# One-token attention on one core: the first pair's odd keys and its values in one load each, and 88 instructions of TensorE ahead of its loop

## The chip, the cores and the metric

The kernel runs on one core of a Trainium2 chip. The metric is the device time of one execution in microseconds; the median of several runs is compared. Beside the runs there is one execution taken by the hardware profiler, and all durations below are from it. "Before" is the kernel without the change, "after" the one with it.

## The reference

Attention for one new token. There are 32 query heads, 8 key and value heads (four query heads share one), 65,536 tokens, and a head size of 128, all in bf16:

```python
def reference(q, k, v):
    B, Hq, Sq, D = q.shape
    Hkv = k.shape[1]
    rep = Hq // Hkv
    k = jnp.repeat(k, rep, axis=1)
    v = jnp.repeat(v, rep, axis=1)
    scale = D ** -0.5
    scores = jnp.einsum("bhqd,bhkd->bhqk", q, k) * scale
    p = _softmax(scores, axis=-1)
    return jnp.einsum("bhqk,bhkd->bhqd", p, v)
```

Keys and values are 134 MB each. Every byte of them is read once.

## The kernel before, in words

**Tiling.** A *unit* is a quarter of one key head's tokens, 16,384 of them, as 128 partitions with 128 tokens each. The 32 units are taken as 16 *pairs* (an even and an odd unit, n = 0 and 1); two pairs make a head. A pair has 8.4 MB of keys and 8.4 MB of values.

**TensorE** runs one hardware loop of 16 laps, a pair each (`tensor_engine`, L178; the pair's body is `pe_pair`, L165). Its instructions are written out in full inside the lap: for each unit 16 groups of eight 128x128 transposes of keys (`pe_transposes`, L132), three groups later that group's eight score matmuls (`pe_scores`, L141), and at the lap's end 128 value matmuls for each unit (`pe_values`, L159). That is 768 matmuls a lap, each with its weight load. The same code is executed in every lap, and SyncE hands out semaphore "tokens" (`tokens`, L404) where a lap has fewer loads than the code has waits. Ahead of the loop stand two waits, the transpose of the queries (L181) and one more wait.

**VectorE and ScalarE** copy each transposed group from PSUM to `ktb` (`evict`, L189 and following; three of four on VectorE, L202, the fourth on ScalarE, L200), find the unit's largest score, exponentiate the scores into `pts` (L342) and add up the results (`values_done`, L249). **GpSimd** finds maxima across partitions and, in most pairs, copies the odd unit's keys from `kbuf` to `bbuf` (L208).

**SyncE** issues every load of keys and values, in program order on one queue (`sync_engine`, L393). `kbuf` holds a pair's keys, `bbuf` the odd unit's copy, `vbuf` a pair's values, each once. So a pair's keys can be asked for when the pair before has been transposed out of `kbuf` (`kfree`), and its values when the pair before has used up `vbuf` (`vfree`, which VectorE raises after TensorE's last value matmul). In pairs 1 to 13 the keys are one load (L413) and the values one load (L436). In pair 0 the keys go in four: the even unit's two halves into `kbuf`, the odd unit's two halves into `bbuf` (`K_PIECES`, L402), each half with a semaphore of its own; the values go in two, one for each unit (L433). TensorE waits for each half at the transposes that begin it, and for each unit's values at the first of its value matmuls. The last two pairs are cut up in their own way, and the change leaves them as they are.

Of the kernel before, what the change touches and what calls it, by code (L numbers as in the profile page):

```python
# [14 lines left out]
NTB = 4  # L15
NKG = 8
LAG = 3
CB = 16
HU = 4
Q = 32  # L20
# [18 lines left out]
def starts(sizes):  # L39
    return [sum(sizes[:i]) for i in range(len(sizes))]  # L40


def take(e, sem, n=1):

    e.wait_ge(sem, n)
    e.sem_inc(sem, -n)  # L46


def bass_standalone__gqa_softmax__decode_kernel(nc, q, k, v, out):
    _, Hq, _, D = q.shape  # L50
    _, H, Sk, _ = k.shape
# [3 lines left out]
    NP = NU // 2  # L55
# [7 lines left out]
    def sb(name, shape, dt):  # L63
        return S(nc.sbuf_tensor(name, shape, dt))

    def sem(name):
        return S(nc.semaphore(name))
# [3 lines left out]
    vbuf = sb("vbuf", [P, 2 * T * D], DT.bfloat16)  # L71
# [34 lines left out]
    vp = [[sem(f"vp{i}_{p}") for p in range(len(V_PIECES[i]))] for i in range(2)]  # L106
# [5 lines left out]
    qkd, qrdy, pvd = sem("qkd"), sem("qrdy"), sem("pvd")  # L112
    cm, cma, ng, dmr, exd, sx, lrd, lra = (sem(n) for n in ("cm", "cma", "ng", "dmr", "exd", "sx", "lrd", "lra"))
    acr, l_sem, lws = sem("acr"), sem("l_sem"), sem("lws")
    xd, xa, xg = sem("xd"), sem("xa"), sem("xg")
    q_sem, o_sem, s_x, t_if, t_id, t_o, t_f, t_row = (
        sem(n) for n in ("q_sem", "o_sem", "s_x", "t_if", "t_id", "t_o", "t_f", "t_row"))

# [5 lines left out]
    def pe_transposes(pe, n, j):  # L124
        kv = (bbuf if n else kbuf)[:, 0:T * D].rearrange("p (t d) -> p t d", d=D)
        if j * TB in starts(K_PIECES[n]):
            take(pe, kp[n][starts(K_PIECES[n]).index(j * TB)], 16)
        if n and j * TB % CB == 0:
            take(pe, cpa if j * TB // CB in sum(ACT_COPIES.values(), ()) else cpg)
        for i in range(TB):  # L130
# [4 lines left out]
    def pe_scores(pe, n, j):  # L135
        take(pe, eva if on_act(j) else evd)
        if n == 0 and j == 0:
            take(pe, qrdy)
        for i in range(TB):
            t, off = j * TB + i, (j % NKG * TB + i) * P  # L140
            ins = pe.matmul(qkb[n][:, t * R:(t + 1) * R], lhsT=ktb[:, off:off + P],  # L141
                            rhs=qcur[:, :], start=True, stop=True)
        if j == G - 1:
            ins.then_inc(qkd, 1)
# [20 lines left out]
    def pe_pair(pe, lap):  # L165
        pend = []
        for n in range(2):
            for j in range(G):
                pe_transposes(pe, n, j)
                pend.append((n, j))  # L170
                if len(pend) > LAG:
                    pe_scores(pe, *pend.pop(0))
        while pend:
            pe_scores(pe, *pend.pop(0))
        for n in range(2):
            pe_values(pe, n, lap)

    def tensor_engine(pe):  # L178
        pe.wait_ge(q_sem, 16)
        pe.wait_ge(t_id, 1)  # L180
        pe.transpose(qps[:, 0:HR], qsb[:, :], ident[0:HR, 0:HR]).then_inc(s_x, 1)  # L181
        pe.wait_ge(t_if, 1)
        with pe.Fori(0, NP) as lap:
            pe_pair(pe, lap)
        pe.wait_ge(t_f, H)
        pe.transpose(trb[0][0:R, 0:P], oT[:, HR - R:HR], ident[:, :]).then_inc(s_x, 1)  # L186
# [17 lines left out]
    def copy_unit(e, cond, copies, op, done, x):  # L204
        with e.If(cond):
            for c in copies:
                off = T * D + c * CB * D
                ins = op(bbuf[:, c * CB * D:(c + 1) * CB * D], kbuf[:, off:off + CB * D])  # L208
                if c != copies[-1]:
# [183 lines left out]
    def sync_engine(e):  # L393
        W = T * D

        def src(x, p):
            h, c = p // 2, p % 2
            return x[h, c * 2 * P * T:(c + 1) * 2 * P * T, :].rearrange("(p t) d -> p (t d)", p=P)

        def pieces(to, s, sizes, sems):  # L400
            for a, w, sm in zip(starts(sizes), sizes, sems):
                e.dma_start(to[:, a * D:(a + w) * D], s[:, a * D:(a + w) * D]).then_inc(sm, 16)  # L402

        def tokens(sems):  # L404
            for sm in sems:
                e.sem_inc(sm, 16)

        for p in range(NP):
            ks, vs = src(kf, p), src(vf, p)
            if p:  # L410
                e.wait_ge(kfree, 3 * p)
            if WHOLE[0] <= p < WHOLE[1]:
                e.dma_start(kbuf[:, :], ks).then_inc(kp[0][0], 16)  # L413
                tokens(kp[0][1:])
            else:
                for n in range(2):
                    if n and p:
                        e.wait_ge(bfree, p)
                    to, s = bbuf if n else kbuf, ks[:, n * W:(n + 1) * W]
                    if p == 0 or (p == NP - 1 and n == 0):  # L420
                        pieces(to, s, K_PIECES[n], kp[n])
                    else:
                        e.dma_start(to[:, 0:W], s).then_inc(kp[n][0], 16)
                        tokens(kp[n][1:])
                e.sem_inc(cpg, len(POOL_COPIES))
                e.sem_inc(cpa, len(sum(ACT_COPIES.values(), ())))
            if p:
                e.wait_ge(vfree, p)
            if WHOLE[0] <= p < WHOLE[1]:
                tokens(kp[1])  # L430
            if p == 0:
                for n in range(2):
                    e.dma_start(vbuf[:, n * W:(n + 1) * W], vs[:, n * W:(n + 1) * W]).then_inc(vp[n][0], 16)  # L433
                tokens(vp[1][1:])
            elif p < NP - 1:
                e.dma_start(vbuf[:, :], vs).then_inc(vp[0][0], 16)  # L436
                tokens(vp[1])
            else:
                for n in range(2):
                    pieces(vbuf[:, n * W:(n + 1) * W], vs[:, n * W:(n + 1) * W], V_PIECES[n], vp[n])  # L440
        e.wait_ge(t_o, H)
        for b, rows in enumerate(OUT_ROWS):
            for r, n in zip(starts(rows), rows):
                e.dma_start(of[r:r + n, b * Q:(b + 1) * Q],
                            orow[b * Q + r:b * Q + r + n, :]).then_inc(o_sem, 16)
        e.wait_ge(t_row, 1)
        e.dma_start(of[HR - R:HR, :], lrow[:, :]).then_inc(l_sem, 16)

    with nc.Block() as block:
        block.tensor(tensor_engine)  # L450
        block.vector(vector_engine)
        block.scalar(scalar_engine)
        block.gpsimd(gpsimd_engine)
        block.sync(sync_engine)
# [30 lines left out]
```

## Time and profile before

| | us |
|---|---|
| median of 3 runs (lowest to highest) | 628.47 (628.29 to 628.52) |
| the profiled execution, its own time | 628.32 |
| its span, first to last instruction | 626.9 |
| TensorE busy with matmuls, all laps | 483.5 |
| VectorE busy | 315.1 |
| ScalarE busy | 229.1 |
| GpSimd busy | 159.9 |

How to read the lines that the prediction shows: the page's slices cut the span into 40 equal parts, and a digit is the busy share in tenths. A queue's row has its packets, megabytes and the share of 16 DMA engines' time. In a row of instructions in order of time stand the start, the length, the engine, the line, the operation, what it writes and reads, the count that was merged into the row, and in brackets how long the engine stood idle before it and what ended that; "issue" means that it waited for nothing that the profile shows, "PEq" that its own sequencer held it. A row of a stretch has, for each engine, the busy time and the number of instructions, then TensorE's granted clock, the share of the DMA engines, and GB/s. In a row of one line's instructions stand the shortest, median and longest duration in ns, and the first and last start. `PEldq` and `SPq` are the sequencers of TensorE and SyncE.

### The profile page before, as it was taken

The numbers are of one execution on the slowest core, as the hardware profiler recorded it, in microseconds if no ns is written. First come the engines' busy times: TensorE is split into PE (matmuls) and PEld (weight loads), VectorE is DVE, ScalarE is ACT, GpSimd is POOL, SyncE is SP. The second block draws the span as 40 slices with busy tenths as digits, with TensorE's granted clock in tenths as the row PEclk, the third lists the DMA queues.
The fourth block names the chain that finished last, engine by engine and source line by source line (L and its number), as shares of the span: only waits on it lengthen the run. The fifth ranks groups of instructions, "written<-read, shape, count | busy, mean of one in ns | idle before, by whom it ended". The sixth has DMA issues, their size and how long they took to land. (4 is left out here: it accounts for less than half of the span.)

```text
span 626.9 us, 27836 instructions
## 1 busy us (share of the span) xinstructions
PE 483.5 (77%) x12292; PEld 477.2 (76%) x12292; DVE 315.1 (50%) x699; ACT 229.1 (37%) x445; POOL 159.9 (25%) x124
## 2 busy tenths in 40 slices
PE   4753995949859598694976949679596894999798
PEld 4752995949859498694976949679596794999798
DVE  4530653717437174471744718346182561848274
ACT  2330542515335153340634407245071441624133
POOL 0000704307042070520605115060150702400000
PEclk9975886959869597795977959779596895969697
DMA  8999999999999999999999999999999999999997
GB/s 368 433 454 424 439 431 439 431 439 426 443 414 456 410 439 426 443 426 439 431 426 444 426 443 426 439 431 439 431 439 431 435 435 435 416 441 426 414 435 310
DMA packets 6424, 268.57 MB, mean 428 GB/s; under 512 B 912, under 2 KB 1040, under 8 KB 1168
## 3 DMA queue, kind: packets, MB, share of 16 engines
q1 hardware_dynamic: 6368, 268.45, 99.2%
q8 instruction: 6, 0.10, 0.1%
q10 hardware_dynamic: 48, 0.01, 0.0%
q14 instruction: 2, 0.02, 0.0%
HBM read 268.44 MB, written 0.01 MB: 428 GB/s over the span
## 5 line engine op out<-in xcount | busy, mean ns | idle before, releaser
L202 DVE COPY ktb<-trb 128x1024 bf16<-128x1024 bf16 x384 | 254.8, 689 | 178.2 <-PE trb L132 173.5
L200 ACT ACTIVATE ktb<-trb 128x1024 bf16<-128x1024 bf16 x128 | 131.1, 1024 | 352.4 <-PE trb L132 296.4
L132 PE MATMUL trb<-ident,kbuf 128*128 128x128 bf16 x2048 | 176.8, 244 | 104.7 <-PEq L46 104.7
L132 PEld LDWEIGHTS trb<-ident,kbuf 128*128 128x128 bf16 x2048 | 143.5, 110 | 105.7 <-issue 105.5
L208 POOL COPY bbuf<-kbuf 128x2048 bf16<-128x2048 bf16 x78 | 143.9, 1893 | 178.2 <-POOLq L46 178.2
L141 PE MATMUL qkb<-qcur,ktb 128*128 128x4 bf16 x4096 | 174.3, 165 | 12.5 <-PEq L46 10.0
L141 PEld LDWEIGHTS qkb<-qcur,ktb 128*128 128x128 bf16 x4096 | 155.7, 97 | 19.0 <-issue 19.0
L132 PE MATMUL trb<-ident,bbuf 128*128 128x128 bf16 x2048 | 156.9, 219 | 4.6 <-issue 4.0
L159 PE MATMUL pvb<-pts,vbuf 128*128 128x4 bf16 x4096 | 112.7, 166 | 14.9 <-issue 9.2
L159 PEld LDWEIGHTS pvb<-pts,vbuf 128*128 128x128 bf16 x4096 | 110.7, 102 | 16.4 <-issue 15.9
L132 PEld LDWEIGHTS trb<-ident,bbuf 128*128 128x128 bf16 x2048 | 117.3, 97 | 1.6 <-issue 1.6
L388 POOL PARTITION_ALL_REDUCE cmaxa<-cmax x32 | 11.8, 370 | 253.8 <-POOLq L46 253.8
L342 ACT ACTIVATE pts<-qkb,negm 128x128 bf16<-128x128 f32 x128 | 51.1, 552 | 37.2 <-ACTq L46 37.2
L351 ACT ACTIVATE bbuf<-kbuf 128x2048 bf16<-128x2048 bf16 x26 | 49.5, 1902 | 0.0
L342 ACT ACTIVATION_READ_ACCUMULATOR pts<-qkb,negm 128x1 f32 x128 | 35.8, 279 | 0.0
L220 DVE TENSOR_REDUCE cmax<-qkb 128x4 f32<-128x512 f32 x32 | 22.0, 687 | 23.1 <-DVEq L46 23.1
L254 DVE TENSOR_TENSOR acc<-acc,pvb 128x4 f32<-128x4 f32 x16 | 2.5, 159 | 31.4 <-PE pvb L159 31.4
L390 POOL PARTITION_ALL_REDUCE la<-lp x8 | 3.4, 430 | 30.5 <-POOLq L46 30.5
L252 DVE COPY acc<-pvb 128x4 f32<-128x4 f32 x8 | 1.3, 162 | 19.5 <-PE pvb L159 19.5
L231 DVE SCALAR_TENSOR_TENSOR negm<-cmaxa,m 128x4 f32<-128x4 f32 x24 | 3.9, 164 | 11.7 <-DVEq L46 11.5
L346 ACT ACTIVATE alpha<-dm 128x4 f32<-128x4 f32 x32 | 7.1, 222 | 0.0
L245 DVE TENSOR_TENSOR acc<-acc,alpha 128x4 f32<-128x4 f32 x24 | 3.9, 163 | 6.1 <-DVEq L46 5.7
(42 smaller groups left out, 39.0 us busy)
## 6 DMA issues: line engine op xcount, KB each, us to landing
vbuf<-in_v_dram SPq DMA_DIRECT2D x3, 4096.0 KB, 30.9
kbuf<-in_k_dram SPq DMA_DIRECT2D x4, 2048.0 KB, 15.9
bbuf<-in_k_dram SPq DMA_DIRECT2D x2, 4096.0 KB, 20.2
bbuf<-in_k_dram SPq DMA_DIRECT2D x2, 2048.0 KB, 19.2
kbuf<-in_k_dram SPq DMA_DIRECT2D x1, 4096.0 KB, 16.3
vbuf<-in_v_dram SPq DMA_DIRECT2D x1, 2336.0 KB, 27.1
vbuf<-in_v_dram SPq DMA_DIRECT2D x1, 1216.0 KB, 29.6
vbuf<-in_v_dram SPq DMA_DIRECT2D x1, 416.0 KB, 30.1
```

Of the source, the lines that this page charges most:

```text
L132: ins = pe.transpose(trb[j % NTB][:, i * P:(i + 1) * P], kv[:, t, :], ident[:, :])
L141: ins = pe.matmul(qkb[n][:, t * R:(t + 1) * R], lhsT=ktb[:, off:off + P], rhs=qcur[:, :], start=True, stop=True)
L159: ins = pe.matmul(pvb[n][:, 0:R], lhsT=vv[:, t, :], rhs=pts[n][:, t * R:(t + 1) * R], start=t == 0, stop=t == T - 1)
L200: e.activation(dst, trb[j % NTB][:, :], AF.Copy).then_inc(eva, 1)
L202: e.tensor_copy(dst, trb[j % NTB][:, :]).then_inc(evd, 1)
L208: ins = op(bbuf[:, c * CB * D:(c + 1) * CB * D], kbuf[:, off:off + CB * D])
L220: e.tensor_reduce(cmax[:, :], qkb[n][:, :].rearrange("p (t g) -> p g t", g=R), AX.X, ALU.max).then_inc(cm, 1)
L231: return e.scalar_tensor_tensor(to[:, :], cmaxa[:, :], -scale, mo[:, :], ALU.mult, ALU.min)
L342: ins = e.activation(pv[:, g, :], sv[:, g, :], AF.Exp, bias=negm[:, g:g + 1], scale=scale, accum_out=rsum[:, g:g + 1])
L346: e.activation(alpha[:, :], dm[:, :], AF.Exp, scale=1.0).then_inc(sx, 1)
L351: return e.activation(o, i, AF.Copy)
L388: e.partition_all_reduce(cmaxa[:, :], cmax[:, :], P, bass.bass_isa.ReduceOp.max).then_inc(cma, 1)
```

## The change

Three edits. In pair 0 the odd unit's keys come in one load into `bbuf` instead of two halves; its second semaphore gets a token from SyncE right after the issue. In pair 0 the values of both units come in one load, with tokens for the second unit's semaphores, as in pairs 1 to 13. And TensorE executes 88 semaphore increments and decrements, once, in front of everything else it does; nobody waits for that semaphore. They stand ahead of the loop in TensorE's program, so that the whole loop begins 88 instructions later in it. The number of SyncE's instructions stays the same: two loads fewer, two tokens more. No other engine's instructions change, and inside TensorE's loop nothing does. Line numbers after it are larger by 3 to 6 up to the loads.

```diff
@@ -15,6 +15,9 @@
 LAG = 3
+
+
+PE_LEAD = 88
 CB = 16
@@ -112,7 +115,7 @@
-    xd, xa, xg = sem("xd"), sem("xa"), sem("xg")
+    xd, xa, xg, lead = sem("xd"), sem("xa"), sem("xg"), sem("lead")
@@ -176,6 +179,9 @@
     def tensor_engine(pe):
+        for _ in range(PE_LEAD // 2):
+            pe.sem_inc(lead, 1)
+            pe.sem_inc(lead, -1)
         pe.wait_ge(q_sem, 16)
@@ -417,7 +423,7 @@
                     to, s = bbuf if n else kbuf, ks[:, n * W:(n + 1) * W]
-                    if p == 0 or (p == NP - 1 and n == 0):
+                    if p in (0, NP - 1) and n == 0:
                         pieces(to, s, K_PIECES[n], kp[n])
                     else:
                         e.dma_start(to[:, 0:W], s).then_inc(kp[n][0], 16)
@@ -428,11 +434,7 @@
-            if p == 0:
-                for n in range(2):
-                    e.dma_start(vbuf[:, n * W:(n + 1) * W], vs[:, n * W:(n + 1) * W]).then_inc(vp[n][0], 16)
-                tokens(vp[1][1:])
-            elif p < NP - 1:
+            if p < NP - 1:
                 e.dma_start(vbuf[:, :], vs).then_inc(vp[0][0], 16)
                 tokens(vp[1])
```

## The prediction

> **What bounds the kernel now.** I read the page's slices and its DMA queues first, then the busy time of chosen stretches, the instructions in order of time for the first pair, and last the chain that ended last.
>
> ```profile
> span 626.9 us, 27836 instructions
> ...
> DMA  8999999999999999999999999999999999999997
> GB/s 368 433 454 424 439 431 439 431 439 426 443 414 456 410 439 426 443 426 439 431 426 444 426 443 426 439 431 439 431 439 431 435 435 435 416 441 426 414 435 310
> ...
> q1 hardware_dynamic: 6368, 268.45, 99.2%
> q8 instruction: 6, 0.10, 0.1%
> ```
>
> The 16 DMA engines are busy in every slice; queue q1, SyncE's loads of keys and values, holds them for 99.2% of the span. 268.45 MB at the 433 GB/s that the row of 100 to 540 us below shows are 620.0 us of the 626.9. The rest is about 2 us of start and, after the last bytes, the closing matmuls:
>
> ```profile
> 620.90 2.09 PE pvb L159 x73
> 622.99 0.43 PE pvb L152 x2
> 623.41 1.58 PE pvb L159 x55
> ```
>
> So the kernel is one unbroken stream of loads with a tail of a few us behind it. A change to the first pair counts only if it alters how fast that stream runs, or tears a hole in it. The first pair, seen from TensorE and SyncE's queue:
>
> ```profile
> 8.26 3.57 PE L132 MATMUL trb<-ident,kbuf 128*128 128x128 bf16 x32 [2.95 <-PEq L46]
> ...
> 20.93 0.21 PE L141 MATMUL qkb<-qcur,ktb 128*128 128x4 bf16 x3 [1.17 <-issue]
> ...
> 21.63 0.46 PEld L132 LDWEIGHTS trb<-ident,bbuf 128*128 128x128 bf16 x8
> ...
> 21.77 0.33 SPq L413 DMA_DIRECT2D kbuf<-in_k_dram  x1
> ...
> 29.25 0.22 PE L132 MATMUL trb<-ident,bbuf 128*128 128x128 bf16 x1 [3.16 <-issue]
> ...
> 36.43 0.56 PE L132 MATMUL trb<-ident,bbuf 128*128 128x128 bf16 x7 [0.81 <-issue]
> ```
> ```profile
> 39.31 1.89 PE L159 MATMUL pvb<-pts,vbuf 128*128 128x4 bf16 x69
> ...
> 46.25 3.53 PE L159 MATMUL pvb<-pts,vbuf 128*128 128x4 bf16 x127 [5.06 <-issue]
> ...
> 53.73 0.27 PE L159 MATMUL pvb<-pts,vbuf 128*128 128x4 bf16 x5 [3.95 <-issue]
> ...
> 54.18 1.71 PE L159 MATMUL pvb<-pts,vbuf 128*128 128x4 bf16 x55 [0.17 <-issue]
> ...
> 56.10 0.33 SPq L436 DMA_DIRECT2D vbuf<-in_v_dram  x1
> 63.06 3.02 PEld L132 LDWEIGHTS trb<-ident,kbuf 128*128 128x128 bf16 x29 [7.27 <-issue]
> ```
>
> In the first pair TensorE stands still five times with no data to wait for ("issue"). Between the last two it does 127 matmuls, with their weight loads 254 instructions. The queue of instructions explains it. Asked for by stretch (0 to 60, 60 to 627, and the two us 18 to 20), its rows are:
>
> ```profile
> q1 hardware_dynamic: 991, 25.10, 98.3%
> q8 instruction: 6, 0.10, 0.6%
> ```
> ```profile
> q1 hardware_dynamic: 5377, 243.35, 99.3%
> q14 instruction: 1, 0.01, 0.0%
> ```
> ```profile
> q8 instruction: 1, 0.02, 3.0%
> ```
>
> All six q8 packets, some 16 KB each, fall in the first 60 us and none later. I read this as TensorE's code being fetched in blocks of about 256 instructions (16 KB by 254 is near 64 bytes each), once, while the first pair runs; from the second pair on the loop is at hand. Each stall is the wait for the next block.
>
> **The change part by part.**
>
> *The stream's own rate.* The odd unit's keys go from two loads with 16 KB per partition to one with 32 KB, the values from two with 32 KB to one with 64 KB. The rates of 16, mostly 32, and 64 KB:
>
> ```profile
> 5.00:20.00 15.00, 11.72 (x214) 11.58 (x215) 8.21 (x16) 3.07 (x3) 0.00 (x0) 1.00 1.01 430
> 20.00:40.00 20.00, 14.41 (x327) 13.96 (x327) 10.39 (x21) 6.61 (x14) 0.37 (x1) 0.91 1.01 431
> 100.00:540.00 440.00, 341.30 (x8695) 337.23 (x8696) 222.63 (x477) 170.91 (x314) 143.09 (x99) 0.78 1.00 433
> ```
>
> 4.19 MB of keys at 430 take 9.75 us, at 431 9.73; 8.39 MB of values at 431 take 19.46, at 433 19.37. Together 0.11 us less. Bounds: nothing, if the lower rates come from the fetches that share these stretches; 0.5 us, if everything from 5 to 60 us ran at 433 (55 us by 0.5%, plus the partly slower start). I take 0.15. [...]
>
> *The 88 instructions.* They are increments and decrements of a semaphore, on TensorE's sequencer, in front of everything it does. The trace has none of these in a row. The nearest rows, below SyncE's first issue, are two waits that follow each other on TensorE, three increments in a row on SyncE, and two neighbours on TensorE's sequencer at the loop's end:
>
> ```profile
> 0.72 0.88 SPq L402 DMA_DIRECT2D kbuf<-in_k_dram  x2
> ```
> ```profile
> L46 PEldq EVENT_SEMAPHORE  x2: 51/51/51, 605.0 to 605.2; - x2
> ```
> ```profile
> L406 SPq EVENT_SEMAPHORE  x3: 17/17/17, 4.0 to 4.1; - x3
> ```
> ```profile
> L183 PEldq ALU_OP  x16: 36/36/42, 55.4 to 624.8; - x16
> L183 PEldq COMPARE_BRANCH  x16: 67/208/219, 55.5 to 624.9; - x16
> ```
>
> TensorE's 51 ns alone is the lower end: 4.5 us. Start to start of the two waits, 0.2, is the upper: 17.6 us. SyncE's are some 0.05 apart with 17 ns each; TensorE's two neighbours 0.1. I take 0.1, TensorE's own row without a wait: 8.8 us. From about 0.7 us, when SyncE's first issue shows the engines begun, TensorE then reaches the queries' transpose at 9.5 and the first keys at about 9.8, not 8.26: +1.5 us. All of the front up to 8.26 is hidden, by the first keys that TensorE waited for (2.95 us). Behind the 88 stand all of TensorE's instructions, and for those wait VectorE's evictions and SyncE's second key load (21.77 before). That load then goes out at about 23; its data follow K0 and V0, 16.8 MB or 39 us of stream, so it has some 17 us to spare.
>
> *Where the code stalls.* 88 instructions are 44 matmuls: each block ends 44 matmuls earlier in the loop. The stalls among the values come after 25 and 152 of the 256 instead of 69 and 196. After the last boundary 104 matmuls are left, 208 instructions and a handful more: still inside that block, so the number of fetches stays six.
>
> *The waits.* Landings before:
>
> ```profile
> L402 SPq DMA_DIRECT2D bbuf<-in_k_dram x2: 419/543/667, 1.7 to 2.1; - x2
> ...
> DMA to landing us min/median/max: 16.3/19.2/22.1
> ```
> ```profile
> L433 SPq DMA_DIRECT2D vbuf<-in_v_dram x2: 442/471/500, 3.0 to 3.5; - x2
> ...
> DMA to landing us min/median/max: 21.9/26.9/40.1
> ```
>
> The odd unit's first half landed at about 18.0, the second at 24.2. In one load all of it is there at 24.2. Before, TensorE began on it at 21.63; now it comes about 1.5 later, at 23.1, and waits 1 us more. That wait lies beside the fetch of the next block, whose stall (3.16 before) shrinks by as much. The values of both units landed by 43.6 (3.5 and 40.1). Before, the even unit's began at 39.31 on the half that was there; now they begin at 43.7. But before, they stopped at 41.2 until 46.25 for code. Now that block is asked for earlier, and is there or nearly there after 25 matmuls, at 44.4 to 46. The next, 152 values in, comes 7.5 us later (46.25 to 53.73 before), at 52 to 53.5. Then 104 matmuls at 31 ns (1.71 by 55) are 3.2 us and the release of the buffer 0.2: the second pair's values are asked for at 55.5 to 57, against 56.10.
>
> *What hides it.* That load stands behind the second pair's keys:
>
> ```profile
> kbuf<-in_k_dram SPq DMA_DIRECT2D x1, 41.2
> ```
>
> Issued at 21.77 they land at 63.0. The first slices of 0.125 us (0 to 5 us) show the lag from an issue to its bytes:
>
> ```profile
> DMA  0000000000000599007030039969099390993909
> ```
>
> From SyncE's issue at 0.72 to the first busy slice it is about 1 us. With that lag, and the engines not all done at the same moment, a request up to about 60 leaves no hole. So the cover is 3 to 4.5 us. The next lap begins on those keys at 63.06, after 7.27 us of idling, so all the shifts of TensorE end there. Every us by which the request comes after 61 makes the end about 1 us later.
>
> **Sum:** the stream −0.15, TensorE's first pair 0. The profiled run took 628.32 (span 626.9 and 1.4 around it): 628.17. The median of the runs is 0.15 above it, so **628.3 us**.
>
> **The rivals.**
> 1. *The front is too long, and the stream runs dry* (slower). At 0.2 us each the front ends at 18.3. Of the 9 us beyond my forecast some 2 to 3 vanish in the waits for landings, so the request comes at 62 to 65 and the hole is 1 to 4 us: 629.3 to 632.3. It decides from about 0.15 us per instruction. For it: the waits' 0.2. Against: those two each had a wait to clear.
> 2. *Two code fetches on one DMA engine.* One fetch takes an engine 0.96 us (3.0% of 16 engines by 2 us). If the shifted fetches met on one engine, its share of the stream would end 1 us later: 629.3. For it: the fetches come at other times. Against: their number is the same.
> 3. *The loop no longer stays at hand* (slower). The five block waits (14.2 us by the rows above) are what makes the first pair's 47.8 us of TensorE (8.26 to 56.10) longer than the 38.8 us of its data (16.8 MB at 433). In all 15 other laps that would be 9 us each: 763 us. For it: the loop ends further on. Against: it ends in the same block as before. [...]
> [...]
> 5. *The code is not moved, or the fetches are not tied to blocks:* then the values start at 43.7 and still meet a 5 us stall, the request comes at about 58, and the time is 628.3 all the same.
>
> **How the numbers follow.** Forecast 0.85 (rival 5 inside it), rival 1 0.09, rival 2 0.03, rival 3 0.01, rival 4 0.02. About 0.2%, or 1.26 us, is what a measurement can tell from no change. Rival 2 stays inside it, and so does a third of rival 1. Faster 0.02, same 0.90, slower 0.08. The range runs from the faster end of the stream's price (628.47 − 0.5, less a little for the runs' spread) to the smaller holes of rival 1 and all of rival 2: 627.8 to 629.8. What is left out is the larger hole and rivals 3 and 4, under 0.1.
>
> **What would show it.** Right: TensorE's first key transpose at 9 to 11 us; the "issue" idles after about 25 and 152 values; the values starting at 43 to 45; the second pair's values asked for by 58; DMA at 9 in every slice; six q8 packets, all before 62 us. Wrong: a slice near 62 us under 9, with the request after 61 (rival 1); q8 packets in later laps (rival 3). What would make me wrong most easily is the price of the 88 instructions, which no row shows.

## The result, and the profile after

| | before | after |
|---|---|---|
| median of 21 runs, us (lowest to highest) | 628.44 (628.18 to 629.79) | 629.58 (628.39 to 630.35) |
| the profiled execution, us | 628.32 | 629.34 |
| its span, us | 626.9 | 628.0 |

After takes 1.0017 times as long as before (95% interval 1.0010 to 1.0023). That is 1.1 us, and it is real: all but three of after's 21 times are 629.34 or more, and all but one of before's are 628.61 or less. I had forecast 628.3 and no change. (629.58 lies inside the range that I gave, 627.8 to 629.8, only because I had set its upper end by the smaller holes of rival 1.)

The page of after, the lines that answer to those of before:

```profile
span 628.0 us, 27924 instructions
...
DMA  8999999999999999999999999999999999999996
...
q1 hardware_dynamic: 6080, 268.45, 99.1%
q8 instruction: 6, 0.10, 0.1%
```

The span is 1.1 us longer, and the 40 slices do not show where: a slice is 15.7 us. Three closer views do. First the front, where TensorE's 88 semaphore instructions are two lines (after, by line; shortest, median and longest ns, then first and last start), and the first transposes behind them (after, in order of time):

```profile
L183 PEldq EVENT_SEMAPHORE  x44: 51/51/51, 0.8 to 14.0; - x44
L184 PEldq EVENT_SEMAPHORE  x44: 51/51/51, 1.0 to 14.1; - x44
```
```profile
14.34 0.10 PEld L187 LDWEIGHTS pvb<-ident,qsb 32*128 32x128 bf16 x1 [14.34 <-issue]
14.67 1.54 PE L135 MATMUL trb<-ident,kbuf 128*128 128x128 bf16 x13
```

Each is shown as 51 ns long, but 88 of them fill 0.8 to 14.1 us: 0.151 us from start to start. The keys' first transposes stand at 14.67, 6.4 us later than before's 8.26. Second, the values of the first pair and the request that follows them (after, in order of time):

```profile
46.81 0.81 PE L162 MATMUL pvb<-pts,vbuf 128*128 128x4 bf16 x25
...
48.45 3.53 PE L162 MATMUL pvb<-pts,vbuf 128*128 128x4 bf16 x127 [0.83 <-issue]
...
55.92 2.92 PE L162 MATMUL pvb<-pts,vbuf 128*128 128x4 bf16 x104 [3.94 <-issue]
...
59.06 0.33 SPq L438 DMA_DIRECT2D vbuf<-in_v_dram  x1
```

The code now stalls after 25 and 152 values instead of 69 and 196. The second pair's values are asked for at 59.06, against 56.10. Third, the 6 us in which the keys asked for earlier end and those values should take over (stretch 60 to 66 us; the last number is GB/s, the one before it the share of the DMA engines, where a packet counts in the stretch in which it starts, so that a share can be over 1). Before, then after:

```profile
60.00:66.00 6.00, 2.90 (x28) 2.94 (x29) 1.53 (x3) 0.00 (x0) 1.57 (x1) 0.50 1.06 459
```
```profile
60.00:66.00 6.00, 3.07 (x30) 3.10 (x31) 1.70 (x3) 0.00 (x0) 1.74 (x1) 0.50 0.94 374
```

459 GB/s become 374. Six us hold only some 40 packets of 64 KB, and each counts where it starts, so this view finds the place but overstates the loss: from 60 to 80 us the rate is 417 against 426, which is 0.2 MB or 0.4 us of stream. The times of the packets are a closer measure (worked out from the trace's packet records). Before, no engine stands idle between 57 and 68 us, and one packet of 64 KB takes longer than 2.8 us where 2.42 is usual. After, the engines stand idle for 0.09 us on the mean, and nine packets take 2.8 to 4.0 us. "The hole" below means both, idle engines and long packets. The digits of 15.7 us hide it. Afterwards the stream runs as before (433 GB/s from 100 to 540 us in both), and the q8 packets of the code (after, 0 to 60 and 60 to 66 us) are still six, the last one inside the hole:

```profile
q8 instruction: 5, 0.08, 0.5%
```
```profile
q8 instruction: 1, 0.02, 1.1%
```

### The profile page after: what moved, and what is told of

Read it like the earlier page. It is cut to its first block, busy times and chain, and to the rows that moved or that the text cites. A ratio compares the mean times of both kernels' runs of the same rounds, so it can differ in the third digit from the quotient of the medians.

```text
span 628.0 us, 27924 instructions
## 1 busy us (share of the span) xinstructions
PE 486.4 (77%) x12292; PEld 480.7 (77%) x12292; DVE 315.3 (50%) x699; ACT 229.1 (36%) x445; POOL 160.1 (25%) x124
## 5 line engine op out<-in xcount | busy, mean ns | idle before, releaser
L135 PE MATMUL trb<-ident,kbuf 128*128 128x128 bf16 x2048 | 178.7, 246 | 99.0 <-PEq L49 98.3
L135 PEld LDWEIGHTS trb<-ident,kbuf 128*128 128x128 bf16 x2048 | 145.2, 112 | 100.1 <-issue 99.9
## 6 DMA issues: line engine op xcount, KB each, us to landing
vbuf<-in_v_dram SPq DMA_DIRECT2D x1, 2336.0 KB, 27.1
```

The costliest lines, as they stand in the source:

```text
L135: ins = pe.transpose(trb[j % NTB][:, i * P:(i + 1) * P], kv[:, t, :], ident[:, :])
```

## The experiments

The theory after the result: the long front makes the request late, the stream runs dry at about 61 us and starts again unevenly. The rivals: the shifted code blocks cost something by themselves; the loads in one piece do; the code fetches hold the loads up where two meet. An expectation gives its theories their letters; where a letter comes without words it is one that an expectation further up has defined. Times are medians of all runs of a kernel; ratios are to runs of before on the same chip, whose medians were 628.2 to 628.3 us. "The request" is SyncE's issue of the second pair's values in the run that was profiled.

### One part alone: the 88 instructions

lead_only is before with the front alone, all loads cut as before:

```diff
     def tensor_engine(pe):
+        for _ in range(PE_LEAD // 2):
+            pe.sem_inc(lead, 1)
+            pe.sem_inc(lead, -1)
         pe.wait_ge(q_sem, 16)
```

> The kernel before with the 88 semaphore instructions alone; the loads of the first pair stay cut up. Theory A (the front is too long: 88 at 151 ns put TensorE's first key transpose at 14.6 us, the second pair's values are asked for too late and the stream of loads has to start anew): first transpose at 14.6, request at 58 to 60 instead of 56.1, DMA packets around 60 us longer than 2.42 us, time 629.0 to 629.8. Theory B (the code's new place: a code fetch meets the stream at a bad moment, however long the front is): the same time. Theory C (the loads in one piece hold the values back until 43.6 us): 628.4, as before.

Measured: 628.35 us (628.14 to 630.78, 12 runs), ratio 1.0005 (0.9997 to 1.0014). Eight of the twelve lie at 628.14 to 628.45, four at 629.15 to 630.78: the same program has two outcomes. The profiled execution was one of the four, 629.77 us. Its values, its request and its stretch from 60 to 66 us:

```profile
44.81 0.77 PE L160 MATMUL pvb<-pts,vbuf 128*128 128x4 bf16 x25
48.65 3.53 PE L160 MATMUL pvb<-pts,vbuf 128*128 128x4 bf16 x127 [3.07 <-issue]
```
```profile
59.24 0.33 SPq L440 DMA_DIRECT2D vbuf<-in_v_dram  x1
```
```profile
60.00:66.00 6.00, 2.83 (x28) 2.86 (x28) 1.46 (x3) 0.00 (x0) 1.50 (x1) 0.50 0.96 352
```

So the front alone puts the request at the same edge, but in the median of its runs it costs nothing: four of twelve take 629.15 us or more, against 18 of 21 that take 629.34 or more with the loads changed as well. The same program was profiled once more, to catch the other outcome:

> The 88 semaphore instructions alone again, one look. Late request as the cause: 628.1 to 628.5 with the request before 58.5 us, or 629.1 and more with the request after 59.

Measured: 628.26 us. The same three views:

```profile
42.87 0.81 PE L160 MATMUL pvb<-pts,vbuf 128*128 128x4 bf16 x25
46.48 3.53 PE L160 MATMUL pvb<-pts,vbuf 128*128 128x4 bf16 x127 [2.79 <-issue]
```
```profile
56.53 0.33 SPq L440 DMA_DIRECT2D vbuf<-in_v_dram  x1
```
```profile
60.00:66.00 6.00, 2.94 (x29) 2.98 (x30) 1.57 (x3) 0.00 (x0) 1.61 (x1) 0.50 1.04 448
```

This pair is the cleanest of the study, since nothing in the program differs. Request 59.24: 352 GB/s in the hole and 629.77. Request 56.53: 448 GB/s and 628.26. What set them apart is in the trace's q8 packets: the third to fifth were at 36.4, 46.2 and 53.8 us in the first of the two executions, at 35.3, 43.9 and 51.0 in the second. A 64 KB packet of the loads takes 2.42 us; the first execution's fourth fetch came about one such turn later, which I read as its place in the queue.

### One part alone: the loads

loads_only is after with `PE_LEAD = 0`; keys_one and values_one are before with one of the two loads each:

```diff
 # loads_only
-PE_LEAD = 88
+PE_LEAD = 0
 # keys_one
-                    if p == 0 or (p == NP - 1 and n == 0):
+                    if p in (0, NP - 1) and n == 0:
 # values_one
-            if p == 0:
-                for n in range(2):
-                    e.dma_start(vbuf[:, n * W:(n + 1) * W], vs[:, n * W:(n + 1) * W]).then_inc(vp[n][0], 16)
-                tokens(vp[1][1:])
-            elif p < NP - 1:
+            if p < NP - 1:
```

> The changed kernel with no instructions in front: the loads of the first pair in one piece alone. Theory A: request for the second pair's values at 55 to 57.5, stream whole, time 628.2 to 628.5. Theory B: the same. Theory C: request near 59, time 629.3 or more.

Measured: 631.17 us (630.22 to 632.47, 6 runs), ratio 1.0045 (1.0033 to 1.0057). The loads in one piece, without the front, are the worst of the three parts. Why, in order of time (loads_only, TensorE, then SyncE's request, then the stretch):

```profile
24.13 1.01 PE L135 MATMUL trb<-ident,bbuf 128*128 128x128 bf16 x8 [2.48 <-PEq L49]
...
33.99 0.22 PE L135 MATMUL trb<-ident,bbuf 128*128 128x128 bf16 x1 [4.18 <-issue]
...
44.16 1.97 PE L162 MATMUL pvb<-pts,vbuf 128*128 128x4 bf16 x69
50.83 3.53 PE L162 MATMUL pvb<-pts,vbuf 128*128 128x4 bf16 x127 [4.71 <-issue]
```
```profile
60.68 0.33 SPq L438 DMA_DIRECT2D vbuf<-in_v_dram  x1
```
```profile
60.00:66.00 6.00, 3.63 (x49) 3.57 (x47) 1.95 (x4) 0.00 (x0) 1.83 (x2) 0.50 0.91 341
```

TensorE waits for the odd keys until 24.1, and the stall for code that follows does not shrink: it was 3.16 us before and is 4.18 here. So wait and fetch come one after the other. It comes to the values at 44.16 instead of 39.31, with no wait in front of them, and after 69 of them stands still for 4.71 us. The request is 4.6 us later than before, when the first engines have ended their keys (from 60.4 us on), and the stream runs dry.

> The kernel before with the odd unit's keys of the first pair in one load, nothing else. Theory D (the values in one load are what delays: their 64 KB packets, queued from 21 us on, hold up the code fetch that TensorE asks for at 20.8 us, served at 31.5 with both loads in one piece and at 26.9 before, and the even unit's values wait until 43.6): here the values stay cut up, the fetch is served near 27, the request for the second pair's values comes by 58, time 628.1 to 628.6. Theory E (the odd keys in one load delay: TensorE waits for all of them until 24.1 us): request after 59, time 629.5 to 631.5.

> The kernel before with the first pair's values in one load, nothing else. Theory D: the code fetch asked for at about 20.8 is served only at 30 to 32 us, the request for the second pair's values comes at 59.5 to 61, time 629.5 to 631.5. Theory E: fetch and request as before, time 628.1 to 628.6.

> The odd keys in one load again, one look. Late request as the cause: 628.2 to 628.5 with the request before 58.5 us, or 629.4 and more with the request after 59.

Measured: keys_one 629.65 us (628.14 to 631.11, 10 runs), ratio 1.0020 (1.0009 to 1.0031), request 60.63 in a run of 630.84; profiled again as keys_one_b, request 60.80 and 630.6 us. values_one 630.91 us (630.78 to 632.13, 4 runs), ratio 1.0047 (1.0030 to 1.0063), request 60.69. Each of the two loads alone made the request as late as both together in the executions profiled, though three of keys_one's ten runs lie at 628.14 to 628.40. keys_one came out by theory E; values_one has the time and the request of theory D, but not its late second fetch. In values_one (TensorE, in order of time) the wait for all values comes first, then the code:

```profile
43.90 1.98 PE L159 MATMUL pvb<-pts,vbuf 128*128 128x4 bf16 x69 [1.85 <-PEq L46]
51.12 3.53 PE L159 MATMUL pvb<-pts,vbuf 128*128 128x4 bf16 x127 [5.24 <-issue]
```

Do larger packets hold the fetches up? In values_one the second fetch was served at 27.1 us, as in before (26.9), so not there. But the third came at 36.4 instead of 34.1, one packet's turn later, although TensorE had met no new wait until then, and its stall grew from 0.81 to 3.14 us. So the larger packets may have a part in the late request; how large a part, beside the wait for all the values, no run shows.

### The code moved, without the long front

lead_mm is after with 44 matmuls (each with its weight load, so 88 instructions) in place of the 88; they work on the identity and write a PSUM bank that the values overwrite later:

```diff
-        for _ in range(PE_LEAD // 2):
-            pe.sem_inc(lead, 1)
-            pe.sem_inc(lead, -1)
-        pe.wait_ge(q_sem, 16)
         pe.wait_ge(t_id, 1)
+        for _ in range(44):
+            pe.matmul(pvb[0][:, 0:R], lhsT=ident[:, :], rhs=ident[:, 0:R], start=True, stop=True)
+        pe.wait_ge(q_sem, 16)
```

> The changed kernel with 44 matmuls (88 instructions with their weight loads) in place of the 88 semaphore instructions; their output is overwritten later. The code of the loop lies where the change puts it, but the front takes some 5 us and ends before the first keys land. Theory A: first transpose at 8.3, request at 55 to 57, time 628.2 to 628.5. Theories B and C: as the change, 629.3 to 629.8.

Measured: 628.03 us (627.92 to 628.22, 11 runs), ratio 0.9995 (0.9987 to 1.0004). TensorE, the request and the stretch of lead_mm:

```profile
3.27 1.34 PE L184 MATMUL pvb<-ident 128*128 128x4 bf16 x44 [3.27 <-DVE ident L325]
```
```profile
8.02 3.57 PE L135 MATMUL trb<-ident,kbuf 128*128 128x128 bf16 x32 [2.95 <-PEq L49]
...
46.11 3.54 PE L162 MATMUL pvb<-pts,vbuf 128*128 128x4 bf16 x127 [1.67 <-issue]
...
53.32 2.91 PE L162 MATMUL pvb<-pts,vbuf 128*128 128x4 bf16 x103 [3.66 <-issue]
```
```profile
56.44 0.33 SPq L437 DMA_DIRECT2D vbuf<-in_v_dram  x1
```
```profile
60.00:66.00 6.00, 3.18 (x31) 3.21 (x32) 1.81 (x3) 0.00 (x0) 1.85 (x2) 0.50 1.03 448
```

The 44 matmuls end at 4.6 us, and the first keys are transposed at 8.02, when they have landed. This is the change as I had pictured it: the same place of the loop, a front that hides behind the first landing. The stall among the values is 1.67 us instead of 4.71, because its fetch now runs beside the wait for the values (it came at 43.75 us, in loads_only at 48.5); the request is back at 56.44 and the stream has no hole. All its times lie below before's median of 628.27, though the interval of the ratio still takes in 1.

The steps in order: before 628.27; the loads alone 631.17 (+2.9); the code moved behind a short front 628.03 (−3.1); that front made 13.3 us long, 629.3 (+1.3; after was measured on another chip, so this is its ratio of 1.0017 times 628.27).

### The request alone

Here nothing but the request is moved: SyncE executes 26, 52 or 104 semaphore instructions between its wait for the buffer and the load, 0.06 us each:

```diff
+            if p == 1:
+                for _ in range(13):        # sp_15; 26 in sp_30, 52 in sp_60
+                    e.sem_inc(late, 1)
+                    e.sem_inc(late, -1)
```

> The kernel before, with 52 semaphore instructions of SyncE (about 57 ns each, 3.0 us) between its wait for the values' buffer and the second pair's value load. TensorE's program, its code and the first pair's loads stay as they are. Theory A: request at 59.1, stream restarts, time 629.0 to 629.6 (the mean of the engines late by 0.4 us, the last one by up to 1). Theories B and C: 628.4, as before. If it comes out near 628.8, the restart alone is worth 0.4, and the rest of the change's loss is the code fetch at 60.6 us that meets it.

> The kernel before, with 26 semaphore instructions of SyncE (1.5 us) between its wait for the values' buffer and the second pair's value load: request at 57.6. Theory A with its edge where the run with 3.0 us put it (59.1 is partly too late): packets around 60 us at 2.42 us, time 628.2 to 628.5. If the edge lies earlier, under 57.6: 628.6 to 629.2. The theories by code place have nothing to add: 628.3.

> The same with 104 semaphore instructions (6.0 us): request at 62.1, after the keys of the second pair have drained. Theory A: a hole of some 3 us on the engines that are done first, about 1.5 on the last, time 630 to 632. If the time stays under 629.5 the request's moment is not what the end hangs on.

Measured: sp_15 628.38 us (628.15 to 629.88, 10 runs), ratio 1.0007 (0.9997 to 1.0016); sp_30 629.21 us (628.20 to 631.65, 12 runs), ratio 1.0016 (1.0005 to 1.0027); sp_60 630.72 us (630.48 to 631.23, 5 runs), ratio 1.0039 (1.0025 to 1.0053). Request and stretch of sp_15, sp_30 and sp_60:

```profile
57.42 0.33 SPq L440 DMA_DIRECT2D vbuf<-in_v_dram  x1
```
```profile
60.00:66.00 6.00, 3.03 (x29) 3.06 (x30) 1.66 (x3) 0.00 (x0) 1.70 (x1) 0.50 1.01 437
```
```profile
59.10 0.33 SPq L440 DMA_DIRECT2D vbuf<-in_v_dram  x1
```
```profile
60.00:66.00 6.00, 2.94 (x29) 2.98 (x30) 1.57 (x3) 0.00 (x0) 1.61 (x1) 0.50 0.88 339
```
```profile
62.30 0.33 SPq L440 DMA_DIRECT2D vbuf<-in_v_dram  x1
```
```profile
60.00:66.00 6.00, 2.91 (x28) 2.94 (x29) 1.54 (x3) 0.00 (x0) 1.58 (x1) 0.50 0.54 187
```

With TensorE, its code and all loads left as before, a request near 59.1 makes the hole and, in the median, the loss; one near 57.4 does not, though two of sp_15's ten runs took 629.70 and 629.88. So a late request is a sufficient cause, and the edge lies between. Theories by which the loss needs the moved code or the larger loads are out; whether these add to it is not shown.

How deep is the hole? In all these runs the engines end the second pair's keys from 60.4 to 60.6 us (the first engine) until 62.2 to 62.5 (the last). The packets between 57 and 68 us say the rest (worked out from the trace's packet records; idle time and excess are means over the 16 engines, the excess being what packets of 64 KB took beyond 2.42 us):

| | request, us | idle, us | packets over 2.8 us | their excess, us | that execution, us |
|---|---|---|---|---|---|
| before | 56.10 | 0.00 | 1 | 0.04 | 628.32 |
| lead_mm | 56.44 | 0.00 | 1 | 0.03 | 628.04 |
| sp_15 | 57.42 | 0.00 | 2 | 0.07 | 628.15 |
| lead_44 (next section) | 58.34 | 0.03 | 9 | 0.68 | 628.58 |
| after | 59.06 | 0.09 | 9 | 0.43 | 629.34 |
| sp_30 | 59.10 | 0.30 | 10 | 0.65 | 630.83 |
| loads_only | 60.68 | 0.76 | 15 | 0.71 | 631.10 |
| sp_60 | 62.30 | 2.08 | 17 | 0.69 | 630.97 |

The harm begins between 57.42 and 58.34, some 2 to 3 us before the first engine has ended its keys, and at first it is packets that take longer (lead_44: 0.68 us of excess) more than engines that stand idle (0.03). The hole and the time go together, but not one for one: sp_60 misses 2.8 us of stream and its execution took 2.65 us longer than before's; sp_30 misses 0.95 and took 2.5 longer, lead_44 misses 0.7 and took 0.3 longer. The 16 completions of the last load of values, one for each DMA engine, show why (worked out from the trace's semaphore events, us):

| | first engine | median | last engine |
|---|---|---|---|
| before | 622.86 | 623.38 | 624.57 |
| lead_mm | 622.70 | 623.20 | 624.33 |
| after | 623.18 | 624.05 | 625.60 |
| sp_30 | 623.60 | 624.34 | 627.10 |
| sp_60 | 626.52 | 626.65 | 627.23 |

The last engine sets the end, and 560 us after the restart the engines are still apart in a way that differs by kernel. In sp_60, where the whole stream stood still, the first ends 3.7 us later than before and the last only 2.7: they lie closer together. In sp_30 the first ends 0.7 later and the last 2.5: they lie further apart. After is a mild case of that, 0.3 and 1.0. I read this as engines that are held up unequally at the restart and never make it up; the table shows the spread, not which engine was late at the restart.

### Other lengths and kinds of front

lead_44 is after with `PE_LEAD = 44`. mm_15 and code_200 are lead_mm with 15 and 100 matmuls (30 and 200 instructions). mm_f32 keeps the long front but makes it of matmuls in float32, each of which is four instructions (before's one float32 matmul, L152, stands in the trace as two matmuls and two weight loads): 22 of them, shown as 44 matmuls, are 88 instructions.

```diff
 # lead_44
-PE_LEAD = 88
+PE_LEAD = 44
 # mm_15 (against lead_mm; 100 in code_200)
-        for _ in range(44):
+        for _ in range(15):
 # mm_f32 (against after, in place of the 88)
+        pe.wait_ge(t_if, 1)
+        for _ in range(22):
+            pe.matmul(pvb[0][:, 0:R], lhsT=identf[:, :], rhs=identf[:, 0:R], start=True, stop=True)
```

> The changed kernel with 44 semaphore instructions instead of 88: at 151 ns each the front ends at 7.4 us, before the first keys land. Theories A and F: first transpose at 8.1, the code fetch for the values' second block asked for ahead of the wait, request at 56 to 58, time 628.0 to 628.6. If the semaphore instructions cost something beside their time on TensorE, it stays over 629. Theory G: 629.4 to 630.

> The changed kernel with 15 matmuls (30 instructions) in front in place of the 88 semaphore instructions: the code moved by a third as much, the front shorter than the wait for the first keys. Theory F (the next block of code is asked for only when TensorE is about half way through the present one, 128 instructions in; in the unmoved loop the wait for the values stands 13 instructions ahead of that point, so the fetch cannot begin before the values have landed at 43.6): 30 instructions move the point 17 ahead of that wait, the fetch is served by 44 instead of 48.5, the request comes at 56 to 58.5, time 628.0 to 628.8. Theory G (the fetch is asked for on entering the block, and the gain grows with the distance moved): a third of the way from 631.2 to 628.0, so 629.8 to 630.6.

> The changed kernel with 100 matmuls (200 instructions) in front in place of the 88: the loop now ends some 70 instructions into one more block. Rival 3 of the prediction (a loop of that length no longer stays at hand): instruction packets in every lap, several stalls of 2 to 5 us in each, time far above, 640 to 770. If the loop stays at hand also so: seven or eight instruction packets, all in the first 70 us, time 628 to 631.

> The changed kernel with 22 matmuls in float32 (two weight loads and two matmuls each, so 88 instructions again) in front in place of the 88 semaphore instructions; their output is overwritten later. The code lies where the change puts it and no semaphore instruction is added, but the front is long: some 0.5 us for each by the one float32 matmul at the loop's end, so 11 us from 3.7, the first transpose at 14 to 15 us. Theory A: request for the second pair's values at 58 to 60, time 629 to 630.4, like the change. If semaphore instructions as such, and not TensorE's late start, make the change slow: 628.0, like the front of 44 short matmuls.

Measured: lead_44 628.27 us (628.08 to 631.45, 10 runs), ratio 1.0005 (0.9993 to 1.0017), request 58.34 in a run of 628.58, just past the expected 56 to 58. Half the instructions end at about 7.4 us (44 by 0.151 from 0.8 on), before the first keys land: TensorE waits another 0.24 us for these and begins on them at 8.08. Eight of ten runs are near before's time. mm_15 631.14 us (628.12 to 634.34, 10 runs), ratio 1.0047 (1.0027 to 1.0066), request 63.23 in a run of 631.56: theories F and G both missed it. In mm_15 (TensorE) a code stall of 3.48 us comes some way behind the wait for the odd keys, and one of 3.58 stands later inside their transposes:

```profile
24.01 1.01 PE L135 MATMUL trb<-ident,bbuf 128*128 128x128 bf16 x8 [3.14 <-PEq L49]
...
33.84 0.32 PE L144 MATMUL qkb<-qcur,ktb 128*128 128x4 bf16 x7 [3.48 <-issue]
...
43.71 0.55 PE L135 MATMUL trb<-ident,bbuf 128*128 128x128 bf16 x5 [3.58 <-issue]
```

So the place of a block's edge beside the waits matters by 3 us (mm_15 631.14, lead_mm 628.03), and I can't say beforehand which place is good. code_200 took 630.01 us (628.73 to 631.59, 10 runs), ratio 1.0027 (1.0018 to 1.0037). It was meant to push the loop over one block too many; it has seven q8 packets, and from 60 us on just this one (at 97.5 us, where I had expected all of them by 70):

```profile
q1 hardware_dynamic: 5375, 243.28, 99.4%
q8 instruction: 1, 0.02, 0.0%
```

But by an estimate from the stalls, which stand 256 instructions apart (before: 449, 705 and so on, as told below), the longer front also moves the loop's beginning into the next block, so that the loop covers no more blocks than before. So the run says nothing on how much code stays at hand. mm_f32 took 628.23 us (627.92 to 629.80, 11 runs), ratio 1.0008 (0.9999 to 1.0017), in two groups: six at 627.92 to 628.23, five at 629.50 to 629.80. The execution profiled was one of the five, 629.50, with its request at 61.25, past the expected 58 to 60. Its front (TensorE) is nearly as long as after's:

```profile
3.79 9.52 PE L185 MATMUL pvb<-identf 128*128 128x4 f32 x44 [3.79 <-ACT identf L376]
...
13.38 3.59 PE L135 MATMUL trb<-ident,kbuf 128*128 128x128 bf16 x32
```

With transposes from 13.38 it is at the edge, and falls on either side of it. Two more profiles of the same program were to tell whether the group goes with the request's moment:

> The late float32 front again, one look. Late request as the cause: time 628.2 or less with the request before 58.5 us, or 629.4 and more with the request after 59, and DMA packets of 2.8 us and longer around 60 us in the second case alone. Another cause: time and request do not go together.

> The late float32 front a third time, one look; the same two outcomes.

Measured: request 59.01 and 629.62 us; request 59.07 and 628.53 us. Here the moment alone does not decide: at 59.0 the one execution took 1.4 us longer than before's 628.21 on that chip and the other 0.3. Nor do the long packets, of which both have some (ten and nine over 2.8 us), against what I had expected. Over the 18 profiled executions of all kernels it reads so: with the request at 57.42 or earlier (four) 628.04 to 628.32 us; from 58.3 to 59.5 (seven) 628.53 to 630.83; from 60.6 (seven) 629.5 to 631.56.

## Why the prediction was wrong

Point by point, by its own steps:

- *What bounds the kernel*: right. In every execution of 629 us or more that was profiled, the stream of loads is disturbed at the one place named, near 62 us: 264 to 416 GB/s from 60 to 72 us, against 426 to 437 in those of 628.4 and less.
- *The 88 instructions*, "I take 0.1": mis-sized. They took 0.151 us each, 13.3 us and not 8.8. The row I took, two neighbours on the sequencer, is not a semaphore instruction; a length of 51 ns in the trace was no pace either. Between my bounds of 0.05 and 0.2 the middle was the answer.
- *Where the code stalls*: right. After 25 and 152 values, six fetches. The blocks are right as well: counted from its first one in the trace, the first pair's code stalls in before and in after stand at TensorE's instructions 449, 705, 961, 1217 and 1473, 256 apart.
- *The waits*: their mechanism was there, but later. I had the values beginning at 43.7 on a landing; with the real front TensorE came to them at 46.81, behind the landing, and waited for none. The request came at 59.06, not at 55.5 to 57. TensorE was 6.4 us later than before at the first keys and 7.5 us later at the values; there the stall for code shrank from 5.06 to 0.83 us, so that the request was only 2.96 us later. In lead_mm, whose front is short, it was 56.44, inside my bounds.
- *What hides it*, "a request up to about 60 leaves no hole. So the cover is 3 to 4.5 us": this is the step that failed. The harm begins between 57.42 (sp_15) and 58.34 (lead_44, nine long packets), and in sp_30, with a request at 59.10, so do idle engines and a loss in the median. The cover over 56.10 is thus 1.3 to 3.0 us. By my own 60, the request of 59.06 that the front of 13.3 us led to would have left no hole. I had reckoned with the end of the keys and the lag of the first byte, 1 us; here a request 2.1 us ahead of the first engine's last key (lead_44) was already too late to keep the packets at 2.42 us.
- *The stream's rate*, −0.15: neither borne out nor refuted; lead_mm is 0.24 below before, and its interval takes in no change.
- *Rival 1*, the front too long, "decides from about 0.15": it is what happened, but not by its own sum. At 0.151 us it was on its turning point, where my sum gave no hole yet; it wanted a request at 62 to 65, and the request was 59.06. That its time, 629.3 to 632.3, holds the measured 629.58 is in part luck. I gave it 0.09, because the two waits' 0.2 seemed to be the waits'. That was no reason to put the chance so low when no row showed the instruction and I had set 0.15 as the turning point.
- *Rival 2*, two fetches on one engine: not needed. sp_30 has a loss of this size (0.9 us in the median) with its code at the places of before.
- *Rivals 3 and 4*: neither was seen. After's six q8 packets all come by 60.7 us, none in a later lap; how long a loop may be was not tested, as code_200 covers no more blocks. Rival 4, with 0.02 of the chances, was a fixed price for each load, and no run shows one: lead_mm has two loads less than before, and its median is 0.24 us lower, with an interval that takes in no change.
- *Rival 5*, the code not moved, "the time is 628.3 all the same": wrong. loads_only is just that and takes 631.17, with its request at 60.68 instead of 58. My sum was wrong there: by the rows of before the request comes 16.8 us after the first values (39.31 to 56.10), so values from 43.7 on give 60.5 and not 58. The fetches were not hidden behind TensorE's work here, moved or not: stalls of 0.8 to 5.2 us stand at the block edges of the first pair in the rows above, while the loads hold the DMA engines for 98% of the first 60 us (before 98.3%, after 98.2%).

What stays open: at which instruction of a block the next one is asked for (mm_15 speaks against both places I tried), why the first packets after a late request take up to 4.5 us, and why the engines come back unequally late. That the fetches wait their turn behind packets of the loads is read from their steps of some 2.4 us; values_one, where the values' packets are larger, fits it with its third fetch alone, and smaller packets were not tried. Why one request near 59 costs 0.3 us and another 1.4 (mm_f32's two) is open too.

## What to carry to other kernels

In a kernel bound by one unbroken stream, ask for each load how much earlier it is issued than the queue runs dry, and treat 2 us of margin as used up, not as spare: in these runs 3.0 us ahead of the first engine's last packet were free (sp_15) and 2.1 us were not (lead_44). Price an instruction that no row shows by both bounds, and where the turning point lies between them, give the bad side its full share. Moving code so that a fetch falls beside a wait was worth 3 us here (631.17 to 628.03), but what is used to move it must itself be short or hidden (a front of 13.3 us gave 1.3 us of that back).

## What the runs showed of the hardware

- A semaphore increment on TensorE's queue took 0.151 us from start to start, with 51 ns shown as its length; on SyncE's it took 0.06 (52 of them put sp_30's request 3.0 us later than before's). A matmul of 128x4 with its weight load, two instructions, took 0.03 us (44 in 1.34), so it was the cheaper filler for code.
- The same program's code fetches came at moments that differ by about one 64 KB packet of the loads, 2.42 us (lead_only's fourth: 46.2 or 43.9 us). At an edge that was enough for two outcomes: 56.53 or 59.24 for the same request, 628.26 or 629.77 for the whole.
- A stream that stopped in part lost more than its gap (sp_30: 0.95 us missed, 2.5 us lost): after sp_30's partial stop the last DMA engine ended 2.5 us later than before where the first ended 0.7 later; after sp_60's full one (2.8 us missed, 2.65 lost) they ended within 0.7 us of each other.
- A load asked for too late was slow while the engines hardly stood idle: with lead_44's request at 58.34 and the first engine's keys ended at 60.41, nine packets of 64 KB took 2.85 to 4.5 us instead of 2.42, with 0.03 us of idle time on the mean.
